# Unused products in TensorE's early gaps, and a regrouped hand-over from routing to the first expert

## The chip, the cores and the metric

The kernel runs on one core of one Trainium2 chip. A core has five engines that run their own instruction streams in order and meet through semaphores: PE (TensorE, matrix products), DVE (VectorE), ACT (ScalarE), POOL (GpSimd) and SP (SyncE, which here only issues DMAs). PE writes its results to PSUM, eight banks of 2 KB for each of the 128 partitions, from where the other engines read them. The metric is the time of one execution on the device in microseconds, less is better. Where several executions are timed, the median is given.

## The reference

Block-causal attention over 8x8 heads, and then a mixture of eight experts with a fixed capacity over its output. Cut to what matters:

```python
# attention: q, k, v are (8, 8, 576, 64) fp32
scores = (1 / sqrt(64)) * q @ k.transpose(0, 1, 3, 2)
scores = where(row // 64 >= col // 64, scores, -1e9)
attn = exp(scores - max(scores)); attn = attn / (sum(attn) + 1e-9)
attn_out = attn @ v
# experts: x is (4608, 512), 8 experts, cap = 576 tokens each
x = attn_out.transpose(0, 2, 1, 3).reshape(4608, 512)
logits = x @ w_gate
# (token, expert) pairs are visited from the largest logit down; a pair is
# taken if the token has no expert yet and the expert has fewer than cap
for e in range(8):
    out[assigned == e] = relu(x[assigned == e] @ w1[e]) @ w2[e]
```

w1 is 512x1024 and w2 1024x512 for each expert. Everything is fp32 from outside.

## The kernel before

The 64 heads are worked off as 32 pairs, two heads side by side in the 128 partitions. For a pair, PE computes the scores of a block of 128 rows (L380, in fp16 parts of q and k, `qT`, `kT`, `kS`), DVE takes the row maxima (L405), ACT the exponentials (L416), and POOL divides the probabilities `P` by the row sums (L438). PE then transposes `P` in 128x128 fp32 blocks (L463, in the order of row blocks t=6 to 0), ACT and DVE copy the transposed blocks `PT` out of PSUM (L444, L446), and PE multiplies them with the values `V` (L498). PSUM banks 4 to 7, called `'x'` in the code, hold the transposes and the value products; two pairs of banks, `'S'`, hold the scores.

Behind the attention come the experts. For expert k a search in 14 rounds finds the logit from which on tokens belong to it. A round is a chain over three engines: `ja` on ACT (L760) and `jk` on DVE (L791) count the tokens above trial thresholds, PE adds the counts over the partitions (`tot`, L807), and DVE picks the next thresholds (L810). The routing then turns the result into a list of row indices (`th` L821, `po` L893, `pe` L995, `ix` L1004). POOL gathers the rows of x by indirect DMA into `xg` (L1068), five pieces of 128 rows (the last has 64). For expert 0, PE transposes each piece (`xt`, L1079, eight blocks) and DVE and ACT copy the result into `X`; for the later experts SP issues transposing DMAs from `xg` into `X` (L1094). PE multiplies with w1 in three fp16 products for each of four slices of the 512 inputs (`h`, L1119). ACT writes relu(h) in fp16 as `HH` (L1105), DVE the rest as `HL` (L1107). PE multiplies these with w2 (`y`, L1145 and L1149), ACT scales (L1127) and POOL scatters the rows to the output (L1135). While expert k is multiplied, the rounds and the gather for expert k+1 run between.

`h` is computed in 8 blocks f of 128 hidden units. The 576 rows are cut in two parts: 128 and 448 for expert 0, 256 and 320 for the others. The name `h_f_part` says which block and part. Each block and part has a PSUM bank of its own out of four (tag `g`), and a first matmul that starts the bank anew and a last one that stops it, since 12 matmuls add up there.

Nothing in this order is written out by hand. A planner (`Sched`) holds a list of tasks, each with its engine, a cost in ns and the events that it waits for, plays them forward on a model of the engines, and emits the instruction of the task that can start next by rules of priority. The instruction stream of an engine is the order in which its tasks were emitted, so a cost or a landing time in the model changes the order of the work and nothing else. `x[0]` in the run loop is the planned start of a task, `s.free[T]` the planned time from which PE is free, `s.res['x']` the planned times at which the `'x'` banks come free. While the first gather is under way, PE multiplies constants ten times into an unused tile (`warm`, L968).

Of the kernel before, what the change touches and what calls it, by code (L numbers as in the profile page):

```python
# [8 lines left out]
F32 = mybir.dt.float32  # L9
F16 = mybir.dt.float16  # L10
I32 = mybir.dt.int32
AF = mybir.ActivationFunctionType
OP = mybir.AluOpType
AX = mybir.AxisListType
P = 128

D, A, T, G, S = "DATGS"
# [6 lines left out]
class Sched:  # L24
# [5 lines left out]
    def __init__(s):  # L30
        s.lanes = [0] * 8
        s.free = {e: 0 for e in "DATGS"}
        s.ev = {0: 0}
        s.rt, s.gn, s.tasks, s.now, s.n, s.q, s.hw, s.res, s.shape = 0, 0, [], 0, 0, 0, 0, {}, None

    def add(s, gen, prio, t):
        s.n += 1
# [79 lines left out]
    def run(s):  # L117
        while s.tasks:
            c = []
            for k in s.tasks:  # L120
                best = None
                bias = next((x for x in k[4][2:] if isinstance(x, float)), 0)
                for n, e in enumerate(k[4][0]):
                    t = s.start(k, e)
                    if t is None:
                        break
                    cost = k[4][1][n] if len(k[4][0]) > 1 else k[4][1]
                    b = max(t, s.free[e] if e != S or cost else 0)
                    b += s.TURN if e == T and any(isinstance(x, Shape) and x != s.shape for x in k[4][2:]) else 0
                    if n == 0 or b + cost + bias < best[0] + best[6]:  # L130
                        best = (b, k[0], k[1], k, t, e, cost)
                if best:
                    c.append(best)
            assert c, [(k[4], k[1]) for k in s.tasks]
            c.sort(key=lambda x: x[:3])
            for x in c:
                end = x[0] + x[6]
                if x[6] == 0 or x[0] - x[4] > s.WAIT or not any(y[1] < x[1] and y[5] == x[5] and y[0] < end - (s.ST if x[5] == T else s.SLACK) and y is not x for y in c):
                    break
            else:  # L140
                x = c[0]
            k, e, cost = x[3], x[5], x[6]
            s.now, s.lat, s.xlag, s.eng = x[0] + cost, True, 0, e
            if e != S or cost:
                s.free[e] = s.now
            if e == T:
                s.shape = next((x for x in k[4][2:] if isinstance(x, Shape)), s.shape)
            s.tasks.remove(k)
            k[2], k[3] = s.now, e
            try:  # L150
                op = next(k[5])
            except StopIteration:
                continue
            if not s.lat:
                k[3] = None
            k[2] += s.xlag
            k[4] = op
            s.tasks.append(k)


class Attn:
# [443 lines left out]
    PX, BX = 3, 0.0  # L605
    PR = dict(load_qk=5, load_v=6, split=7, swap=2, scores=5, transpose=6, values=8, rows=7, logits=5, gate=1)

    def start(s):
        sc = s.sc
        sc.res.update(S={0: 0, 1: 0}, x={4: 0, 5: 0, 6: 0, 7: 0})  # L610
        for nm, f in (('load_qk', s.load_qk()), ('split', s.split('q')), ('split', s.split('k')), ('swap', s.swap()), ('load_v', s.load_v()),
                      ('scores', s.scores()), ('transpose', s.transpose()), ('values', s.values()), ('rows', s.rows()), ('logits', s.logits()), ('gate', s.gate())):
            sc.add(f, s.PR[nm], 0)


class Moe:
# [443 lines left out]
    def gather(s,k,ix):  # L1060
        nc=s.nc; fp=s.fp; sc=s.sc
        tl=[]
        for m in range(5):
            n=P if m<4 else 64
            yield G,1038 if k else 1350,('ffn',k-2),('xm',k-1,m)
            if m==0: X=s.X[k]=fp.tile([P,8,576],F16,tag="X",name=f"X{k}")
            xg=fp.tile([P,1024],F16,tag="xg",name=f"xg{k}_{m}",bufs=5)
            nc.gpsimd.indirect_dma_start(out=xg[:n],out_offset=None,in_=s.xd,in_offset=bass.IndirectOffsetOnAxis(ap=ix[:n,m:m+1],axis=0))  # L1068
            sc.soft(728,('xg',k,m))
            if k==0: sc.ev['xg',k,m]=sc.now+3000  # L1070
            sc.nolat()
            if m==4: sc.set(('gi',k))
            sc.add(s.flip(k,m,n,xg,X),1,sc.now)
# [23 lines left out]
    def ffn(s,k):  # L1097
        nc=s.nc; fp=s.fp; sc=s.sc
        yield S,0,('xm',k,0),('xm',k,1 if k else 0),*[('wc',k,n) for n in range(4) if k or n==0]
        (W,Y),X=s.W[k],s.X[k]  # L1100
        HH=fp.tile([P,8,576],F16,tag="HH",name=f"HH{k}",bufs=1); HL=fp.tile([P,8,576],F16,tag="HL",name=f"HL{k}",bufs=1)
        def hev(f,h,ps,gk,ts):
            w=ts.stop-ts.start
            yield A,51+.835*w
            nc.scalar.activation(HH[:,f,ts],ps,AF.Relu)  # L1105
            yield D,69+1.042*w
            nc.vector.scalar_tensor_tensor(HL[:,f,ts],ps,0.0,HH[:,f,ts],op0=OP.max,op1=OP.subtract)  # L1107
            sc.set(('h',k,8*h+f)); sc.set(gk)
        for h,ts in enumerate((slice(0,256),slice(256,576)) if k else (slice(0,128),slice(128,576))):
            w=ts.stop-ts.start  # L1110
            for f0 in range(0,8,4):
                pg={}
                nf=4 if k==0 and h==0 and f0==0 else 1
                for f,d in [(f,d) for a in range(f0,f0+4,nf) for d in range(4) for f in range(a,a+nf)]:
                    yield T,3*(w/2.4+3),'g' if d==0 else None,('g2',k-1),*[('xm',k,m) for m in range(1,5) if h],('wc',k,d) if k==0 else None
                    if d==0: gk=sc.gtake(); pg[f]=s.ps.tile([P,512],F32,tag="g",name=f"h{k}_{f}_{h}",bufs=4)[:,:w],gk
                    ps,gk=pg[f]
                    for n,(a,l) in enumerate(((0,0),(0,2),(1,0))):
                        nc.tensor.matmul(ps,lhsT=W[:,a,d,f*P:f*P+P],rhs=X[:,4*(d//2)+d%2+l,ts],start=(d==0 and n==0),stop=(d==3 and n==2))  # L1119
                    sc.nolat()  # L1120
                    if d==3: sc.add(hev(f,h,ps,gk,ts),1,sc.now+200)
        sca=1.0/(s.XS*s.WS*s.WS)
        def yev(m,ps,gk):
            n=P if m<4 else 64
            yield A,478
            y=fp.tile([P,512],F32,tag="y",name=f"yo{k}_{m}",bufs=3)
            nc.scalar.activation(y[:n],ps[P-n:],AF.Copy,scale=sca)  # L1127
            if m==4:

                yield D,603  # L1130
                nc.vector.scalar_tensor_tensor(y[:n],ps[:n],sca,y[:n],op0=OP.mult,op1=OP.add)
            sc.set(gk)

            yield G,1038,('yo',s.ny-1),('gi',1) if k==0 and m>1 else None
            nc.gpsimd.indirect_dma_start(out=s.out,out_offset=bass.IndirectOffsetOnAxis(ap=s.ix[k][:n,m:m+1],axis=0),in_=y[:n],in_offset=None)  # L1135

            if m==4 and k>s.E-3: nc.gpsimd.drain()
            sc.soft(728,('yo',s.ny)); sc.ev['yo',s.ny]=max(sc.ev['yo',s.ny],sc.now+4500); s.ny+=1
        for m in range(5) if k+1<s.E else (0,1,2,4,3):
            if m==0: sc.set(('mid',k))  # L1140
            for f in range(8 if m<4 else 4):
                yield T,645 if m<4 else 720,*[(x,k,y) for g in ((f,) if m<4 else (f,f+4)) for x,y in (('h',g),('h',8+g),('wc',4+g//2))],'g' if f==0 else None
                if f==0: gk=sc.gtake(); ps=s.ps.tile([P,512],F32,tag="g",name=f"y{k}_{m}",bufs=4)
                for n,(Z,a) in enumerate(((HH,0),(HH,1),(HL,0))):
                    if m<4: nc.tensor.matmul(ps,lhsT=Z[:,f,m*P:m*P+P],rhs=Y[:,a,f],start=(f==n==0),stop=(f==7 and n==2))  # L1145
                    else:

                        for g in range(2):
                            nc.tensor.matmul(ps[64*g:64*g+64],lhsT=Z[:,4*g+f,512:576],rhs=Y[:,a,4*g+f],start=(f==n==0),stop=(f==3 and n==2))  # L1149
                sc.nolat()  # L1150
            if m==4: sc.set(('g2',k)); sc.set(('ffn',k))
            sc.add(yev(m,ps,gk),1,sc.now+200)
        if k+1<s.E: sc.add(s.ffn(k+1),3,sc.now)
# [10 lines left out]
def attention_moe_kernel(ctx, tc, q, k, v, wg, w1, w2, out):  # L1164
    nc = tc.nc
# [5 lines left out]
    x = dram.tile([N, 2 * H * D], F16, name="x")  # L1171
    sc = Sched()
    with tc.manual_schedule():
# [8 lines left out]
            sc.add(moe.consts(), 70, 0)  # L1182
            sc.run()
        with ExitStack() as inner:
            sc.SLACK, sc.ST, sc.WAIT = 150, 500, 300
            moe.pools(inner)
            moe.run()
# [25 lines left out]
```

## Time and profile before

| what | us |
|---|---|
| median of 3 runs | 773.67 (769.49 to 773.80) |
| the profiled execution, whole | 775.91 |
| its span from first to last instruction | 774.1 |

The profile is of one execution. Its span counts from the first instruction to the last, and the 1.8 us more of the whole execution lie around it. One run of three is 4 us faster than the others without any change of the program. The page shows for each engine the time that it is busy; the trace gives start and length of groups of instructions, and in brackets how long the engine was idle before such a group and what ended that wait. PE's granted clock is full or half, and the page shows it by slices.

| stage | us of the span |
|---|---|
| start-up and first head pairs | 0 to 32 |
| attention | 32 to 340 |
| logits' end, routing and gather for expert 0 | 340 to 375 |
| expert 0 and the routing for expert 1 | 375 to 425 |
| experts 1 to 7 | 425 to 774 |

### The profile page before, as it was taken

How to read it: one execution, taken by the hardware profiler on the slowest of the kernel's cores; microseconds unless marked ns; L12 is line 12 of the kernel's file. 1: busy time of each engine (PE TensorE's matmuls, PEld its weight loads, DVE VectorE, ACT ScalarE, POOL GpSimd, SP SyncE). 2: the span in 40 equal slices, each digit the busy share in tenths (PEclk: the TensorE clock that was granted, in tenths of full speed). 3: DMA queues.
4: the chain of work that ended last, by engine and by line, in shares of the span. 5: the costliest groups of instructions: out<-in, count | busy, mean ns of one | idle time of the engine just before them, and what ended most of it. 6: DMA issues, size and time to landing. Idle time of an engine off the chain costs nothing.

```text
span 774.1 us, 18968 instructions
## 1 busy us (share of the span) xinstructions
PE 715.2 (92%) x6496; PEld 475.2 (61%) x6496; DVE 560.7 (72%) x2290; ACT 537.0 (69%) x1451; POOL 467.9 (60%) x515
## 2 busy tenths in 40 slices
PE   5779998999989999966999999999999999999997
PEld 3656776667767777743545747647557475574753
DVE  6899888998889889758988978869678693420210
ACT  5688888888988899844835869594965947492211
POOL 5788977898889886714413447293761926766001
PEclk9899999999999999986999999999999999999999
DMA  9878999999999986245229276492935719752001
GB/s 203 165 151 164 214 196 215 175 152 228 187 214 173 229 195 110 78 118 188 106 80 225 98 245 157 166 204 71 279 88 184 184 40 286 254 157 76 28 14 48
DMA packets 249123, 122.84 MB, mean 159 GB/s; under 512 B 205601, under 2 KB 232097, under 8 KB 249025
## 3 DMA queue, kind: packets, MB, share of 16 engines
q1 hardware_dynamic: 243088, 102.60, 59.2%
q0 software_dynamic: 5936, 19.01, 8.0%
q8 instruction: 52, 0.85, 0.5%
q14 instruction: 47, 0.38, 0.2%
HBM read 71.45 MB, written 18.87 MB: 117 GB/s over the span
## 4 chain that ended last, share of the span: by engine, by line
PE 36%; DMA 8%; ACT 3%; POOL 2%; issue 2%; DVE 1%; SPq 1%; POOLq 0%; ACTq 0%; DVEq 0%
PE h L1119 20%; PE y L1145 13%; DMA raw<-in_moe_w_dram 4%; DMA xg<-x,ix 2%; PE y L1149 2%; DMA out_dram<-yo,ix 1%; DMA X<-xg 1%; POOL xg L1068 1%; ACT ja L760 1%; POOL W L1038 1%; ACT W L1036 1%; ACT raw L1032 1%; SPq L1094 1%; PE pe L995 0%; SPq L1008 0%
## 5 line engine op out<-in xcount | busy, mean ns | idle before, releaser
L438 POOL TENSOR_TENSOR P<-P,m 128x320 f32<-128x320 f32 (+8 forms) x285 | 209.6, 770 | 48.7 <-DVE m L430 32.3
L1119 PE MATMUL h<-X,W 128*128 128x320 f16 (+3 forms) x1536 | 195.5, 286 | 2.1 <-DMA X<-xg 1.9
L1119 PEld LDWEIGHTS <-W 128*128 128x128 f16 x1536 | 141.5, 98 | 43.6 <-issue 4.5
L416 ACT ACTIVATE P<-psb,m 128x576 f32<-128x576 f32 (+8 forms) x288 | 149.4, 543 | 25.8 <-DVE m L409 17.2
L1145 PE MATMUL y<-W,HH 128*128 128x512 f16 x512 | 152.3, 379 | 0.0
L405 DVE TENSOR_REDUCE m<-psb 128x1 f32<-128x576 f32 (+8 forms) x288 | 124.9, 481 | 12.6 <-PE psb L380 12.1
L1038 POOL TENSOR_TENSOR W<-raw,W 128x1024 f16<-128x1024 f32 x56 | 118.3, 2137 | 26.0 <-ACT W L1036 22.5
L463 PE MATMUL psb<-mident,P 128*128 128x128 f32 x800 | 107.3, 283 | 12.5 <-POOL P L438 5.7
L1135 POOL DMA_INDIRECT out_dram<-yo,ix x40 | 39.2, 980 | 115.1 <-ACT yo L1127 69.8
L380 PEld LDWEIGHTS <-qT 128*64 128x64 f16 x1408 | 77.1, 112 | 43.7 <-issue 29.2
L463 PEld LDWEIGHTS psb<-mident,P 128*128 128x128 f32 x800 | 88.5, 144 | 23.9 <-POOL P L438 8.4
L380 PE MATMUL psb<-kT,qT 128*64 128x288 f16 (+8 forms) x704 | 90.7, 284 | 11.1 <-ACT P L416 10.3
L498 PE MATMUL psb<-PT,V 128*64 128x448 f32 (+5 forms) x776 | 98.1, 391 | 2.1 <-DVE PT L446 1.6
L1145 PE MATMUL y<-W,HL 128*128 128x512 f16 x256 | 97.0, 379 | 0.0
L1105 ACT ACTIVATE HH<-h 128x320 f16<-128x320 f32 (+3 forms) x128 | 51.7, 407 | 62.4 <-PE h L1119 57.2
L1068 POOL DMA_INDIRECT xg<-x,ix x40 | 41.0, 1025 | 79.9 <-DMA raw<-in_moe_w_dram 32.2
L444 ACT ACTIVATE PT<-psb 128x512 f32<-128x512 f32 (+1 forms) x165 | 82.5, 593 | 5.3 <-PE psb L463 4.9
L1107 DVE SCALAR_TENSOR_TENSOR HL<-h,HH 128x320 f16<-128x320 f32 (+3 forms) x128 | 57.2, 452 | 37.5 <-ACT HH L1105 37.4
L380 PE MATMUL psb<-kS,qT 128*64 128x288 f16 (+8 forms) x704 | 82.8, 280 | 1.2 <-DVE kS L350 1.0
L1145 PEld LDWEIGHTS <-HH 128*128 128x128 f16 x512 | 46.9, 98 | 53.7 <-issue 2.6
L1032 ACT ACTIVATE raw<-raw 128x512 f32<-128x512 f32 x112 | 67.3, 624 | 9.8 <-DMA raw<-in_moe_w_dram 9.0
L498 PEld LDWEIGHTS psb<-PT,V 128*64 128x64 f32 x776 | 49.7, 138 | 33.3 <-issue 24.4
(239 smaller groups left out, 1027.9 us busy)
## 6 DMA issues: line engine op xcount, KB each, us to landing
raw<-in_moe_w_dram SPq DMA_DIRECT2D x64, 512.0 KB, 5.4
x<-XR SPq DMA_DIRECT2D x8, 1152.0 KB, 5.5
kn<-in_k_dram SPq DMA_DIRECT2D x15, 576.0 KB, 5.1
qn<-in_q_dram SPq DMA_DIRECT2D x15, 576.0 KB, 7.4
V<-in_v_dram SPq DMA_DIRECT2D x64, 128.0 KB, 4.1
V<-in_v_dram SPq DMA_DIRECT2D x16, 64.0 KB, 3.7
xg<-x,ix POOLq DMA_INDIRECT x41, 4.5
out_dram<-yo,ix POOLq DMA_INDIRECT x40, 3.6
```

Of the source, the lines that this page charges most:

```text
L380: nc.tensor.matmul(out if len(K1.shape) == 2 else out.rearrange("p (r j) -> p r j", r=2), lhsT=A[:, h, 64 * i:64 * i + 64], rhs=K1, start= ...
L405: nc.vector.tensor_reduce(m[:, 0, c:c + 1], ps[:, o:o + 64 * (i + 1)] if g else s.part(ps, g, i, o), axis=AX.X if g else AX.XY, op=OP.max)
L416: nc.scalar.activation(out, in_, AF.Exp, bias=m[:, 1, c:c + 1], scale=s.ESC, accum_out=m[:, 2, c:c + 1])
L438: nc.gpsimd.tensor_tensor(sl, sl, m[:, 3, c:c + 1].to_broadcast([P, w]), op=OP.mult)
L444: s.nc.scalar.activation(out, in_, AF.Copy)
L463: nc.tensor.transpose(ps[:, a], s.Pb[n % s.NP][:, s.OFF[i] + 128 * j:s.OFF[i] + 128 * j + P], s.ident)
L498: nc.tensor.matmul(ps[64 * h:64 * h + 64, 64 * (i0 - b0):64 * (b1 - b0)], lhsT=vn[:, j, 2 * (n % 2) + h, :], rhs=pt[:, s.PTI[(j, i0)]:s.PT ...
L1032: nc.scalar.activation(raw[:,x],raw[:,x],AF.Copy,scale=s.WS)
L1038: nc.gpsimd.tensor_tensor(lw,raw,hi,op=OP.subtract)
L1107: nc.vector.scalar_tensor_tensor(HL[:,f,ts],ps,0.0,HH[:,f,ts],op0=OP.max,op1=OP.subtract)
L1119: nc.tensor.matmul(ps,lhsT=W[:,a,d,f*P:f*P+P],rhs=X[:,4*(d//2)+d%2+l,ts],start=(d==0 and n==0),stop=(d==3 and n==2))
L1145: if m<4: nc.tensor.matmul(ps,lhsT=Z[:,f,m*P:m*P+P],rhs=Y[:,a,f],start=(f==n==0),stop=(f==7 and n==2))
```

## The change

Three edits. First, the planner gets a hook `fill`. It is called ahead of a PE task whose planned start lies between 13 and 30 us, if the planned gap on PE holds more than one unit of 215 ns and an `'x'` bank is free. It emits as many products of a 128x128 constant with a 128x512 broadcast of that constant into the free bank, and nothing reads them. It is switched off for the expert part.

```diff
+            if e == T and s.fill and 13000 < x[0] < 30000:
+                n, b = int((x[0] - s.free[T]) / 215), [t for t in s.res['x'] if s.res['x'][t] <= s.free[T]]
+                if n > 1 and b:
+                    s.fill(n, b[-1])
...
+    def fill(s, n, b):
+
+        for _ in range(n):
+            s.nc.tensor.matmul(s.bank(b), lhsT=s.moe.idh, rhs=s.moe.idh[:, None, :].to_broadcast([P, 4, P]), start=True, stop=True)
...
+        sc.fill = s.fill
...
-            sc.SLACK, sc.ST, sc.WAIT = 150, 500, 300
+            sc.SLACK, sc.ST, sc.WAIT, sc.fill = 150, 500, 300, None
```

Second, the planned cost of issuing expert 0's gathers and their planned landing become numbers for each piece:

```diff
-            yield G,1038 if k else 1350,('ffn',k-2),('xm',k-1,m)
+            yield G,1038 if k else (1350,1300,1900,2000,1750)[m],('ffn',k-2),('xm',k-1,m)
...
-            if k==0: sc.ev['xg',k,m]=sc.now+3000
+            if k==0: sc.ev['xg',k,m]=sc.now+(3700,2900,2350,2400,2600)[m]
```

Third, for expert 0's first 128 rows four blocks f share one PSUM bank, so that two evictions of 128x4x128 take the place of eight of 128x128 on ACT and on DVE. Only the first matmul of a bank starts it and only the last stops it:

```diff
-        def hev(f,h,ps,gk,ts):
-            w=ts.stop-ts.start
+        def hev(f,h,ps,gk,ts,nf):
+            w=nf*(ts.stop-ts.start); x=slice(f,f+nf)
             yield A,51+.835*w
-            nc.scalar.activation(HH[:,f,ts],ps,AF.Relu)
+            nc.scalar.activation(HH[:,x,ts],ps,AF.Relu)
             yield D,69+1.042*w
-            nc.vector.scalar_tensor_tensor(HL[:,f,ts],ps,0.0,HH[:,f,ts],op0=OP.max,op1=OP.subtract)
+            nc.vector.scalar_tensor_tensor(HL[:,x,ts],ps,0.0,HH[:,x,ts],op0=OP.max,op1=OP.subtract)
...
-                nf=4 if k==0 and h==0 and f0==0 else 1
+                nf=1 if k or h else 4
                 for f,d in [(f,d) for a in range(f0,f0+4,nf) for d in range(4) for f in range(a,a+nf)]:
+                    new=d==0 and (f-f0)%nf==0
...
+                    if new: gk=sc.gtake(); pf=s.ps.tile([P,512],F32,tag="g",name=f"h{k}_{f}_{h}",bufs=4)[:,:nf*w].rearrange("p (f t) -> p f t",f=nf)
...
-                        nc.tensor.matmul(ps,lhsT=W[:,a,d,f*P:f*P+P],rhs=X[:,4*(d//2)+d%2+l,ts],start=(d==0 and n==0),stop=(d==3 and n==2))
+                        nc.tensor.matmul(ps,lhsT=W[:,a,d,f*P:f*P+P],rhs=X[:,4*(d//2)+d%2+l,ts],start=(new and n==0),stop=(d==3 and n==2 and (f-f0+1)%nf==0))
```

In all, PE gets 20 unused products at four places of the first head pairs; otherwise no engine's order differs in the attention. Line numbers of the kernel after are higher: L380, L463, L498, L807, L1079 and L1119 of before are L384, L467, L502, L817, L1089 and L1130.

The third of the four places, on PE: the 128-wide scores of the second pair (`qT_171` is its q), and behind them the four transposes of row block t=5 of the first pair (`P_88`). Before:

```order
L380 LDWEIGHTS qT_171
L380 MATMUL psb<-kS_114,qT_171 64x128
L380 LDWEIGHTS qT_171
L380 MATMUL psb<-kS_114,qT_171 64x128
L463 MATMUL psb<-mident,P_88 128x128 x4
L380 LDWEIGHTS qT_171
L380 MATMUL psb<-kT_166,qT_171 64x320
```

After (L615 is the hook, `m_idh` the constant):

```order
L384 LDWEIGHTS qT_171
L384 MATMUL psb<-kS_114,qT_171 64x128
L615 LDWEIGHTS m_idh
L615 MATMUL psb<-m_idh 128x512
L615 LDWEIGHTS m_idh
L615 MATMUL psb<-m_idh 128x512
L615 LDWEIGHTS m_idh
L615 MATMUL psb<-m_idh 128x512
L615 LDWEIGHTS m_idh
L615 MATMUL psb<-m_idh 128x512
L467 MATMUL psb<-mident,P_88 128x128 x4
```

Four products now stand between the scores and the transposes. The other places are ahead of the transposes of t=6 of the first pair (4), between the 224-wide and the 512-wide scores of the second pair (7), and ahead of the first value product (5).

The hand-over to expert 0, on PE: before, the first three `h` products stand between the transposes of the gather's second piece (`xg_1`) and its third (`xg_2`). Before:

```order
L1079 LDWEIGHTS xg_1_5755
L1079 MATMUL xt_1_5812<-m_idh,xg_1_5755 128x128
L1119 LDWEIGHTS W_0_5742
L1119 MATMUL h_0_0_5833<-X_5744,W_0_5742 128x128
L1119 LDWEIGHTS W_0_5742
L1119 MATMUL h_0_0_5833<-X_5744,W_0_5742 128x128
L1119 LDWEIGHTS W_0_5742
L1119 MATMUL h_0_0_5833<-X_5744,W_0_5742 128x128
L1079 LDWEIGHTS xg_2_5780
L1079 MATMUL xt_2_5838<-m_idh,xg_2_5780 128x128
```

After:

```order
L1089 MATMUL xt_2_5850<-m_idh,xg_2_5800 128x128
L1089 LDWEIGHTS xg_2_5800
L1089 MATMUL xt_2_5850<-m_idh,xg_2_5800 128x128
L1130 LDWEIGHTS W_0_5762
L1130 MATMUL h_0_0_5869<-X_5764,W_0_5762 128x128
L1130 LDWEIGHTS W_0_5762
L1130 MATMUL h_0_0_5869<-X_5764,W_0_5762 128x128
```

The first `h` products moved behind the third piece. In groups, PE's order up to the first 448-wide product was xt_0, tot_0, xt_1, 3 h, xt_2, 9 h, xt_3, 9 h, xt_4, 6 h, tot_1, and then h with tot_2 behind 21 and tot_3 behind 33 more; it is now tot_0, xt_0, xt_1, xt_2, 12 h, xt_3, 12 h, tot_1, 6 h, xt_4, 27 h, tot_2, 36 h, tot_3, 3 h. These `tot` belong to the search for expert 1.

The start of expert 1, on PE: `y_4` is the end of expert 0, `tot_3` the fourth round of the search for expert 2, and `h_0_0` the first product of expert 1, with its rows `X` and weights `W_1`. Before:

```order
L1149 MATMUL y_4_6659<-W_0_5743,HL_5830 64x512
L807 LDWEIGHTS m_bo
L807 MATMUL tot_3_6705<-cn_3_6678,m_bo 128x3
L1119 LDWEIGHTS W_1_6414
L1119 MATMUL h_0_0_6711<-X_6539,W_1_6414 128x256
```

After:

```order
L1160 MATMUL y_4_6650<-W_0_5763,HL_5860 64x512
L1130 LDWEIGHTS W_1_6422
L1130 MATMUL h_0_0_6709<-X_6547,W_1_6422 128x256
L1130 LDWEIGHTS W_1_6422
L1130 MATMUL h_0_0_6709<-X_6547,W_1_6422 128x256
L1130 LDWEIGHTS W_1_6422
L1130 MATMUL h_0_0_6709<-X_6547,W_1_6422 128x256
L817 LDWEIGHTS m_bo
L817 MATMUL tot_3_6714<-cn_3_6686,m_bo 128x3
```

`tot_3` moved behind the first three products of expert 1. In the later experts `tot` and other small steps stand at other places among the products in the same way.

More of the change, by code (lines that the diff above doesn't have):

```diff
@@ L33, in __init__ @@
         s.ev = {0: 0}
-        s.rt, s.gn, s.tasks, s.now, s.n, s.q, s.hw, s.res, s.shape = 0, 0, [], 0, 0, 0, 0, {}, None
+        s.rt, s.gn, s.tasks, s.now, s.n, s.q, s.hw, s.res, s.shape, s.fill = 0, 0, [], 0, 0, 0, 0, {}, None, None
     def add(s, gen, prio, t):
@@ L1101, in ffn @@
         HH=fp.tile([P,8,576],F16,tag="HH",name=f"HH{k}",bufs=1); HL=fp.tile([P,8,576],F16,tag="HL",name=f"HL{k}",bufs=1)
-        def hev(f,h,ps,gk,ts):
-            w=ts.stop-ts.start
+        def hev(f,h,ps,gk,ts,nf):
+            w=nf*(ts.stop-ts.start); x=slice(f,f+nf)
             yield A,51+.835*w
-            nc.scalar.activation(HH[:,f,ts],ps,AF.Relu)
+            nc.scalar.activation(HH[:,x,ts],ps,AF.Relu)
             yield D,69+1.042*w
-            nc.vector.scalar_tensor_tensor(HL[:,f,ts],ps,0.0,HH[:,f,ts],op0=OP.max,op1=OP.subtract)
-            sc.set(('h',k,8*h+f)); sc.set(gk)
+            nc.vector.scalar_tensor_tensor(HL[:,x,ts],ps,0.0,HH[:,x,ts],op0=OP.max,op1=OP.subtract)
+            for i in range(f,f+nf): sc.set(('h',k,8*h+i))
+            sc.set(gk)
         for h,ts in enumerate((slice(0,256),slice(256,576)) if k else (slice(0,128),slice(128,576))):
@@ L1111, in ffn @@
             for f0 in range(0,8,4):
-                pg={}
-                nf=4 if k==0 and h==0 and f0==0 else 1
+                nf=1 if k or h else 4
                 for f,d in [(f,d) for a in range(f0,f0+4,nf) for d in range(4) for f in range(a,a+nf)]:
-                    yield T,3*(w/2.4+3),'g' if d==0 else None,('g2',k-1),*[('xm',k,m) for m in range(1,5) if h],('wc',k,d) if k==0 else None
-                    if d==0: gk=sc.gtake(); pg[f]=s.ps.tile([P,512],F32,tag="g",name=f"h{k}_{f}_{h}",bufs=4)[:,:w],gk
-                    ps,gk=pg[f]
+                    new=d==0 and (f-f0)%nf==0
+                    yield T,3*(w/2.4+3),'g' if new else None,('g2',k-1),*[('xm',k,m) for m in range(1,5) if h],('wc',k,d) if k==0 else None
+                    if new: gk=sc.gtake(); pf=s.ps.tile([P,512],F32,tag="g",name=f"h{k}_{f}_{h}",bufs=4)[:,:nf*w].rearrange("p (f t) -> p f t",f=nf)
+                    ps=pf[:,(f-f0)%nf]
                     for n,(a,l) in enumerate(((0,0),(0,2),(1,0))):
-                        nc.tensor.matmul(ps,lhsT=W[:,a,d,f*P:f*P+P],rhs=X[:,4*(d//2)+d%2+l,ts],start=(d==0 and n==0),stop=(d==3 and n==2))
+                        nc.tensor.matmul(ps,lhsT=W[:,a,d,f*P:f*P+P],rhs=X[:,4*(d//2)+d%2+l,ts],start=(new and n==0),stop=(d==3 and n==2 and (f-f0+1)%nf==0))
                     sc.nolat()
-                    if d==3: sc.add(hev(f,h,ps,gk,ts),1,sc.now+200)
+                    if d==3 and (f-f0+1)%nf==0: sc.add(hev(f-nf+1,h,pf,gk,ts,nf),1,sc.now+200)
         sca=1.0/(s.XS*s.WS*s.WS)
```

## The prediction

> **What bounds the kernel now.** I read the page's engine shares and clock row first, then busy time by stage, then the clock around each dip, the matmul timeline there, and last the hand-over from routing to the experts. On the page the second number is TensorE's (PE's) share of the span, and PEclk gives the granted clock of each fortieth of it in tenths:
>
> ```profile
> PE 715.2 (92%) x6496; PEld 475.2 (61%) x6496; DVE 560.7 (72%) x2290; ACT 537.0 (69%) x1451; POOL 467.9 (60%) x515
> PEclk9899999999999999986999999999999999999999
> ```
>
> Stretches that I cut at the start-up, the attention, the routing, expert 0 and the other experts; columns: length, busy time of PE, its weight loads, DVE, ACT and POOL, then granted clock, DMA share, GB/s:
>
> ```profile
> 0.00:32.00 32.00, 18.98 (x160) 14.16 (x162) 21.33 (x68) 20.63 (x55) 18.52 (x48) 0.89 0.93 177
> 32.00:340.00 308.00, 287.31 (x3271) 215.00 (x3267) 265.17 (x884) 260.42 (x801) 247.02 (x324) 0.99 0.88 175
> 340.00:375.00 35.00, 19.82 (x232) 12.96 (x230) 30.62 (x146) 17.32 (x41) 10.49 (x12) 0.76 0.67 210
> 375.00:425.00 50.00, 48.09 (x321) 24.67 (x319) 42.86 (x214) 28.47 (x67) 18.25 (x13) 1.00 0.49 114
> 425.00:774.10 349.10, 340.99 (x2521) 208.38 (x2519) 200.69 (x983) 210.15 (x490) 173.59 (x118) 1.00 0.50 144
> ```
>
> PE is the bound at 93% of 32 to 340 and 98% of 425 to 774; it idles in the first 32 us and the 35 us of routing. The change works at these two seams. What it saves there counts only if the PE-bound stretch behind it starts earlier.
>
> The clock first. Windows cut to fit its steps; columns: length, PE busy, granted clock, DMA share, GB/s:
>
> ```profile
> 19.78:23.20 3.42, 1.62 (x14) 1.00 0.26 43
> 23.20:26.61 3.41, 2.40 (x19) 0.50 0.68 130
> 26.61:30.02 3.41, 3.41 (x17) 0.50 1.10 203
> 47.09:50.50 3.41, 1.85 (x26) 1.00 1.06 195
> 50.50:53.92 3.42, 3.42 (x22) 0.50 1.11 260
> 419.14:422.55 3.41, 1.83 (x18) 1.00 1.21 185
> ```
>
> The steps lie on one grid of 3.41 us, whatever the kernel does. A window with PE busy 1.62 or 1.85 us is followed by one at half clock; the page's clock row shows no step behind the 1.83 in 419 to 423. After a full window (26.61 to 30.02, 50.50 to 53.92) the clock is back. So I put the threshold near 1.84 us of work, that is, about 1.57 us of idle within one window.
>
> The matmuls around the first dip (start, duration, in brackets the idle ahead and what ended it), and POOL's normalising beside them:
>
> ```profile
> 18.10 0.33 PE L463 MATMUL psb<-mident,P 128*128 128x128 f32 x1 [0.79 <-POOL P L438]
> 20.92 0.41 PE L380 MATMUL psb<-kT,qT 128*64 128x512 f16 x2 [1.49 <-ACT P L416]
> 22.23 0.44 PE L463 MATMUL psb<-mident,P 128*128 128x128 f32 x2
> 24.09 0.69 PE L463 MATMUL psb<-mident,P 128*128 128x128 f32 x2 [1.42 <-POOL P L438]
> 26.42 4.25 PE L463 MATMUL psb<-mident,P 128*128 128x128 f32 x21
> 31.55 2.92 PE L498 MATMUL psb<-PT,V 128*64 128x128 f32 x24 [0.88 <-DVE PT L446]
> 36.85 2.40 PE L463 MATMUL psb<-mident,P 128*128 128x128 f32 x20
> 22.65 7.00 POOL L438 TENSOR_TENSOR P<-P,m 128x512 f32<-128x512 f32 x9 [2.27 <-DVE m L430]
> ```
>
> At half clock the block of transposes takes 4.25/21 = 202 ns each; at full clock (36.85) 120 ns.
>
> **Part 1: the unused products.** Twenty of 128x512 fp16, at four places: 4 ahead of the transpose at 18.10, 7 ahead of the 512-wide scores at 20.92, 4 ahead of the two transposes at 22.23, 5 ahead of the first value product at 31.55. The nearest row is the y product with 512 columns:
>
> ```profile
> 412.33 0.59 PE L1145 MATMUL y<-W,HH 128*128 128x512 f16 x2
> 412.98 0.59 PE L1145 MATMUL y<-W,HH 128*128 128x512 f16 x2
> ```
>
> Three products (two with HH, one with HL) start between these, 0.65/3 = 0.217 us each. The four groups cost 0.87, 1.52, 0.87 and 1.08 us. The idle they stand in is 0.79, 1.49, 1.42 and 0.88 us, so they overrun by 0.08, 0.03, nothing and up to 0.20. The third group is covered because the next two transposes wait for POOL until 24.09 anyway; without POOL's wait it would cost its 0.87. The products read a constant and write a free bank of PSUM, so no DMA and no other engine works for them, and nothing waits for them but the PE rows behind.
>
> With 19.78 to 23.20 filled, its busy time goes from 1.62 to about 1.62+1.52+0.87, the whole window but for what the phase moves; no step at 23.20. Then the 21 transposes take 21x0.120 = 2.52 us and not 4.25. They still begin at 26.42, because POOL's last multiply of the pair sets that. They end at 28.94; the last PSUM copy ran 0.88 behind, so the values could start at 29.82, and the fifth group's 1.08 us plus the transpose ahead of it (0.12 us) puts it at about 30.2. Against 31.55 that is 1.3 us earlier. Is it kept? The largest of PE's waits in 32 to 340, grouped by what they are for (sum, times, longest):
>
> ```profile
> PE psb L380 <- ACT P L416: 7.3, 15, 1.0
> ```
>
> It is on an engine that moves along with PE; no DMA is among the others. I count the whole **-1.3 us**. Bounds: 0 if a dip stays, -1.7 (21x0.082) if nothing else stood in the way; the value taken lies between, by the values' own start.
>
> The weak point is the grid: it runs free, so its place in another execution is any. Before, nearly every place of a 3.41-us window catches too little work somewhere in 17 to 30. After, only 23 to 26.4 remains thin: 0.6 us idle ahead of 24.09, then some 0.2 ahead of 26.42, and scores that take at full clock half of what they show. A window from about 23.0 to 26.4 holds some 1.7 us and would still trip, which I estimate for a quarter of the places.
>
> [...]
>
> **Parts 2 and 3: the hand-over.** The planned issue costs and landing times of expert 0's gathers emit nothing; they alone reorder. Four blocks per bank make 2 evictions of 128x4x128 on ACT and on DVE out of 8 of 128x128. ACT's by form, with sum in us and mean in ns:
>
> ```profile
> L1105 ACT ACTIVATE HH<-h 128x128 f16<-128x128 f32 x8 | 1.8, 269 | 0.0
> L1105 ACT ACTIVATE HH<-h 128x448 f16<-128x448 f32 x8 | 4.3, 538 | 0.0
> ```
>
> From 128 to 448 columns ACT grows 0.84 ns a column, so 512 take 592 ns, and two of them 1.2 us against 2.2 (8x0.269). DVE has as many evictions of the same shapes, which I take to save as much. Neither is the bound in 375 to 425, so the 1.0 us each only relieves the routing beside them. On PE the order counts:
>
> ```profile
> 366.50 0.62 PE L1079 MATMUL xt<-m_idh,xg 128*128 128x128 f16 x8 [1.02 <-DMA xg<-x,ix]
> 368.45 0.41 PE L1079 MATMUL xt<-m_idh,xg 64*128 64x64 f16 x8 [0.82 <-DMA xg<-x,ix]
> 371.13 0.16 PE L807 MATMUL tot<-cn,m_bo 128*128 128x3 f16 x1 [0.62 <-ACT ja L760]
> 371.41 2.00 PE L1119 MATMUL h<-X,W 128*128 128x128 f16 x33
> 373.27 2.14 PE L1119 MATMUL h<-X,W 128*128 128x128 f16 x21
> ```
>
> 33 h products take 2.00 us, 61 ns each. Before, 81 of the 96 narrow ones stand ahead of the row at 373.27 and 15 follow, so the 448-wide ones start at 373.27+15x0.061 = 374.2. After, the gathers land as before (nothing ahead of them moved), 12 products fit in the gap ahead of 368.45 and 6 more behind tot_1; past 368.86 remain 66, 4.0 us, and two tots whose inputs have arrived: 373.1. So PE is 1.1 us ahead. Is that kept? Rows of the next route and of expert 1's start:
>
> ```profile
> 395.42 0.18 PE L807 MATMUL tot<-cn,m_bo 128*128 128x3 f16 x1
> 406.84 1.00 POOL L1068 DMA_INDIRECT xg<-x,ix x1 [0.77 <-DVE ix L1004]
> 412.90 7.78 DMA X<-xg
> 418.63 0.18 PE L807 MATMUL tot<-cn,m_bo 128*128 128x3 f16 x1
> 420.72 1.80 PE L1119 MATMUL h<-X,W 128*128 128x256 f16 x15 [1.91 <-DMA X<-xg]
> 422.35 0.17 PE L807 MATMUL tot<-cn,m_bo 128*128 128x3 f16 x1
> ```
>
> Expert 1 begins when its gathered rows land, and these hang on route 1, a chain of small steps on ACT, DVE and PE whose rounds keep their pace: I place its last tot at 395.5 to 395.6, not earlier. So the 1.1 us turns into a longer wait: **+0.1**. The wait grows from 1.9 to about 3.2 us, also because tot_3 of route 2, at 418.63 ahead of the wait before, now stands behind three products of expert 1. Route 2's next rounds on ACT and DVE wait for it. A round takes (395.42-371.13)/11 = 2.2 us; from tot_3 at about 421.1 (three products of 1.80/15 = 0.12 us behind 420.72) tot_4 comes at 423.3 and not 422.35, so the route runs about 1 us late. Expert 2's first h stands without a wait at
>
> ```profile
> 471.01 0.83 PE L1119 MATMUL h<-X,W 128*128 128x256 f16 x6
> ```
>
> so up to 1.0 us of wait may appear there; between 0 and 1.0 I take **+0.3**, nearer the lower end because PE did not wait there at all.
>
> A wait of 3.2 us holds over 1.57 us of one window wherever the grid lies, so it trips; the half clock then costs half a window of products, 1.7 us. Before, 1.9 us of wait trips where 1.57 fall in one window, which counted over all places is about 64 in 100. The change adds 0.36x1.7 = **+0.6**.
>
> Sum: -1.3+0.1+0.3+0.6 = -0.3 us. The profiled execution took 775.91 us, 2.2 above the median of 773.67 of the three runs shown; there the sum gives 775.6, and on the median 773.4.
>
> **Rivals.** (1) The hand-over's gain survives: if expert 1's indices are found earlier, because DVE and ACT are relieved by 1.0 us, X lands 1.1 earlier, the wait stays at 1.9 and nothing new trips: -1.3-1.1+0.3 = -2.1, 771.6. Against it: the chain waits for the round before, not for evictions. (2) The fills do nothing for the clock: the dip moves to the thin window ahead of 26.4 and the transposes stay at 202 ns; only the hand-over counts, +1.0, and the time is 774.7. For it: 1.62 and 1.85 tripped. (3) Slower by the clock at expert 1 alone: if before hardly ever trips there, as its 1.83 us of work did not, while 3.2 us of wait always does, the whole 1.7 is new: -1.3+0.4+1.7 = +0.8, 774.5. It decides from 1.57 us of idle in one window. Expert 2's wait at its upper bound adds 0.7 more, 775.2.
>
> **How the numbers follow.** The forecast 0.45, rival 1 0.2, rival 2 0.2, rival 3 0.15. The cases lie between 771.6 and 775.2, closer together than the three runs shown (769.49 to 773.8); since places of the grid differ by whole dips of 1.7 us from run to run, I widen by about 2 below and 1 above: 769.5 to 776.0. A measurement of this kernel tells about 1%, 7.7 us, from no change. Every case is within it: same 0.94, and 0.03 to each side for what I have not seen.
>
> **What would show it.** Right: no half clock between 23 and 30, 21 transposes in about 2.5 us and the first value product 1.3 earlier; 20 new matmuls of 0.22 us; 448-wide products from about 1.1 us earlier against the attention's end; the wait for X about 3 us and a half-clock window behind it. Wrong: a dip one window later than before, an attention that ends no earlier though its start does, X landing earlier, or a wait for X at expert 2.

## The result, and the profile after

The changed kernel took 783.23, 782.45 and 779.46 us; a fourth run, of 3469.35 us, was disturbed and is left out of the ratio, though it counts in the median of 782.84. Before took 773.02 (median of four runs here). The ratio is 1.0114, 95% interval 1.0082 to 1.0146: slower by about 1.1%, where 773.4 and no difference were forecast. The profiled execution is 783.23 us, its span 781.4 against 774.1, so 7.3 us of the loss lie inside the span.

The page's PE row and clock row after:

```profile
PE 719.5 (92%) x6516; PEld 476.5 (61%) x6516; DVE 556.0 (71%) x2284; ACT 536.4 (69%) x1445; POOL 467.0 (60%) x515
PEclk9999999999999999967999997999999999999999
```

The dip of the second slice is gone. A new one stands in slice 25, at 469 to 488 us, where before had none: the seam between expert 1 and expert 2.

First the attention. PE's timeline there (start, duration, and in brackets the idle ahead with what ended it):

```profile
15.93 0.33 PE L384 MATMUL psb<-kT,qT 128*64 128x320 f16 x2 [1.74 <-ACT P L420]
...
25.94 2.72 PE L467 MATMUL psb<-mident,P 128*128 128x128 f32 x21 [1.06 <-POOL P L442]
28.50 1.24 PE L615 MATMUL psb<-m_idh 128*128 128x512 f16 x5
29.67 1.57 PE L502 MATMUL psb<-PT,V 128*64 128x128 f32 x10
```

The 21 transposes took 2.72 us (4.25 before), and the first value product starts at 29.67 instead of 31.55. Of these 1.88 us, 0.48 were there before any unused product (these scores started at 16.41 before), so the products are worth about 1.4 here. In the profile with 33 products, in the last of the runs below, the first value product starts at 29.48.

How early the routing starts is read from the first POOL instruction behind the attention, a memset (first row before, second after, each from POOL's timeline):

```profile
340.71 0.13 POOL L673 MEMSET m_PB<- 128x36 f32 x1 [11.54 <-issue]
```
```profile
337.60 0.13 POOL L683 MEMSET m_PB<- 128x36 f32 x1 [11.55 <-issue]
```

The attention ends 3.1 us earlier: the 1.9 us above, and 1.2 more. Where the 1.2 come from isn't shown. Before has a half-clock window from 132.4 to 135.8 that this execution lacks, but a later run without the unused products lacks it too and has this memset at 341.58. In the nine profiles with the 20 products it lies between 337.35 and 339.39.

The hand-over and the start of expert 1, PE's timeline:

```profile
370.06 2.03 PE L1130 MATMUL h<-X,W 128*128 128x128 f16 x12
...
417.81 0.80 PE L1130 MATMUL h<-X,W 128*128 128x256 f16 x3 [3.17 <-DMA X<-xg]
```

Of the 12 products at 370.06 three are narrow, so the 448-wide ones start at 370.2, 4.0 us before the old 374.2: 3.1 of these come from the attention and 0.9 from the new order. Expert 1 starts at 417.81, 2.9 us earlier. The 0.9 became wait, as forecast.

All of PE's waits between 430 and the end (what for; sum, times, longest). Before, this list had one entry, for tot, 1.7 us in all:

```profile
PE tot L817 <- ACT ja L770: 5.2, 4, 3.0
PE h L1130 <- POOL W L1048: 3.2, 1, 3.2
```

The two long ones stand next to each other, at the start of expert 2:

```profile
472.32 0.16 PE L817 MATMUL tot<-cn,m_bo 128*128 128x3 f16 x1 [2.99 <-ACT ja L770]
472.35 2.51 PE L1130 MATMUL h<-X,W 128*128 128x256 f16 x11
478.06 2.32 PE L1130 MATMUL h<-X,W 128*128 128x256 f16 x10 [3.21 <-POOL W L1048]
```

PE is done with expert 1 and the tot behind it at 469.33, waits 2.99 us for tot_6 of the search for expert 3, and 11 products later 3.21 us for a slice of expert 2's weights. The clock there, in windows cut on its steps (length, PE busy, granted clock, DMA share, GB/s):

```profile
414.35:417.76 3.41, 0.30 (x4) 1.00 0.72 183
417.76:421.17 3.41, 3.35 (x17) 0.50 1.13 177
468.96:472.37 3.41, 0.42 (x7) 1.00 0.71 214
472.37:475.79 3.42, 2.49 (x12) 0.50 0.96 250
475.79:479.20 3.41, 1.14 (x6) 0.50 0.20 77
479.20:482.61 3.41, 3.41 (x19) 0.50 0.00 0
```

One half-clock window behind the wait for X at expert 1, three at expert 2. From expert 1's start to expert 3's it took 530.76-417.81 = 112.95 us, against 521.52-420.72 = 100.80 before. Of these 12.15 us the waits are 3.0+3.2. The half clock is taken to cost half of the busy time in its windows (an h product takes 2.51/11 = 0.23 us at 472.35, and 2.45/21 = 0.12 at full clock in the row of before below): 3.35/2 = 1.7 at expert 1 and (2.49+1.14+3.41)/2 = 3.5 at expert 2. Together that is 11.4; the other 0.8 are not traced. Expert 3 to the end is 1.9 us shorter than before. So -2.9+12.15-1.9 = +7.3, the difference of the spans.

Why a slice of weights comes late is seen in POOL's timeline at that seam, before and after. L1038 and L1048 are conversions of weight slices, L1135 and L1146 scatters of expert 1's output. Before:

```profile
461.30 2.14 POOL L1038 TENSOR_TENSOR W<-raw,W 128x1024 f16<-128x1024 f32 x1
463.60 1.01 POOL L1135 DMA_INDIRECT out_dram<-yo,ix  x1 [0.17 <-ACT yo L1127]
464.64 6.30 POOL L1038 TENSOR_TENSOR W<-raw,W 128x1024 f16<-128x1024 f32 x3
471.11 1.00 POOL L1135 DMA_INDIRECT out_dram<-yo,ix  x1 [0.17 <-issue]
476.20 0.96 POOL L1135 DMA_INDIRECT out_dram<-yo,ix  x1 [4.09 <-ACT raw L1032]
```

After:

```profile
461.02 1.00 POOL L1146 DMA_INDIRECT out_dram<-yo,ix  x1 [0.30 <-issue]
462.05 6.32 POOL L1048 TENSOR_TENSOR W<-raw,W 128x1024 f16<-128x1024 f32 x3
468.53 1.00 POOL L1146 DMA_INDIRECT out_dram<-yo,ix  x1 [0.17 <-ACT raw L1042]
474.89 0.96 POOL L1146 DMA_INDIRECT out_dram<-yo,ix  x1 [5.36 <-ACT ja L770]
475.88 4.21 POOL L1048 TENSOR_TENSOR W<-raw,W 128x1024 f16<-128x1024 f32 x2
```

Before, all four slices of expert 2's first weights are converted by 470.94. PE's products there:

```profile
471.01 0.83 PE L1119 MATMUL h<-X,W 128*128 128x256 f16 x6
471.71 2.45 PE L1119 MATMUL h<-X,W 128*128 128x256 f16 x21
```

The slices are multiplied in order, three products each, and only the third of a slice reads the part that POOL converts. So slice 3 is first needed by the twelfth product, the sixth of the second row, at about 472.3: 1.3 us behind its conversion. After, it is the twelfth product too that waits until 478.06, behind the 11 shown above. The planner now put the scatter of piece 1 ahead of slice 0, and those of pieces 2 and 3 ahead of slice 3. Between the two scatters POOL stands still for 5.36 us, and slice 3 is finished at about 478.0. ACT is named as the releaser, but it had written piece 3 by 467.3; in a later run, where slice 3 stands between the same two scatters, the trace names the write of the scatter before as what the next one waits for (0.23 us). Here the trace has that write landing 5.6 us behind its issue, at 474.1, and the scatter of piece 3 starts 0.8 us behind the landing. The same pause stands in the profile before (4.09 us): the write lands 4.3 us behind its issue, at 475.4, and the next scatter again starts 0.8 us behind that. There, nothing that PE needed at once was queued behind it.

The wait for tot_6 hangs on ACT:

```profile
470.48 0.63 ACT L1042 ACTIVATE raw<-raw 128x512 f32<-128x512 f32 x1 [1.05 <-DMA raw<-in_moe_w_dram]
471.13 0.59 ACT L1138 ACTIVATE yo<-y 64x512 f32<-64x512 f32 x1
471.63 0.55 ACT L770 ACTIVATE ja<-m_PB,cd 128x324 f16<-128x324 f32 x1
```

`ja` of that round is queued behind a conversion step whose raw weights are late, and PE's row of tot_6 now stands ahead of expert 2's first product (before, behind the first six).

### The profile page after: what moved, and what is told of

Its sections match the earlier page's. It is cut to its first block, busy times and chain, and to the rows that moved or that the text cites. A ratio compares the mean times of both kernels' runs of the same rounds, so it can differ in the third digit from the quotient of the medians.

```text
span 781.4 us, 18999 instructions
## 1 busy us (share of the span) xinstructions
PE 719.5 (92%) x6516; PEld 476.5 (61%) x6516; DVE 556.0 (71%) x2284; ACT 536.4 (69%) x1445; POOL 467.0 (60%) x515
## 4 chain that ended last, share of the span: by engine, by line
PE 39%; DMA 5%; ACT 4%; issue 3%; POOL 2%; DVE 2%; POOLq 0%; SPq 0%; ACTq 0%; DVEq 0%
PE h L1130 23%; PE y L1156 12%; DMA raw<-in_moe_w_dram 2%; PE y L1160 2%; ACT W L1046 1%; DMA out_dram<-yo,ix 1%; ACT ja L770 1%; DMA X<-xg 1%; POOL W L1048 1%; ACT raw L1042 1%; PE warm L978 1%; PE pe L1005 1%; POOL xg L1078 1%; DMA xg<-x,ix 1%; ACT yo L1138 0%
## 5 line engine op out<-in xcount | busy, mean ns | idle before, releaser
L1130 PE MATMUL h<-X,W 128*128 128x320 f16 (+3 forms) x1536 | 199.9, 290 | 6.4 <-POOL W L1048 3.2
L1130 PEld LDWEIGHTS <-W 128*128 128x128 f16 x1536 | 143.9, 99 | 51.9 <-issue 4.5
L1048 POOL TENSOR_TENSOR W<-raw,W 128x1024 f16<-128x1024 f32 x56 | 118.1, 2132 | 24.7 <-ACT W L1046 24.1
L467 PE MATMUL psb<-mident,P 128*128 128x128 f32 x800 | 104.9, 279 | 11.5 <-POOL P L442 5.3
L1146 POOL DMA_INDIRECT out_dram<-yo,ix x40 | 39.2, 981 | 118.4 <-ACT yo L1138 71.4
L384 PEld LDWEIGHTS <-qT 128*64 128x64 f16 x1408 | 76.0, 111 | 41.9 <-issue 27.3
L467 PEld LDWEIGHTS psb<-mident,P 128*128 128x128 f32 x800 | 86.5, 141 | 22.9 <-POOL P L442 7.4
L384 PE MATMUL psb<-kT,qT 128*64 128x288 f16 (+8 forms) x704 | 89.4, 281 | 11.4 <-ACT P L420 10.0
L1115 ACT ACTIVATE HH<-h 128x256 f16<-128x256 f32 (+3 forms) x122 | 51.2, 420 | 70.2 <-PE h L1130 63.8
L502 PE MATMUL psb<-PT,V 128*64 128x448 f32 (+5 forms) x776 | 97.2, 388 | 0.9 <-DVE PT L450 0.4
L1117 DVE SCALAR_TENSOR_TENSOR HL<-h,HH 128x256 f16<-128x256 f32 (+3 forms) x122 | 56.6, 467 | 41.5 <-ACT HH L1115 41.4
L384 PE MATMUL psb<-kS,qT 128*64 128x288 f16 (+8 forms) x704 | 81.7, 277 | 0.1
L502 PEld LDWEIGHTS psb<-PT,V 128*64 128x64 f32 x776 | 49.3, 137 | 32.3 <-issue 24.4
```

The lines of the kernel that those rows point to most:

```text
L384: nc.tensor.matmul(out if len(K1.shape) == 2 else out.rearrange("p (r j) -> p r j", r=2), lhsT=A[:, h, 64 * i:64 * i + 64], rhs=K1, start= ...
L467: nc.tensor.transpose(ps[:, a], s.Pb[n % s.NP][:, s.OFF[i] + 128 * j:s.OFF[i] + 128 * j + P], s.ident)
L502: nc.tensor.matmul(ps[64 * h:64 * h + 64, 64 * (i0 - b0):64 * (b1 - b0)], lhsT=vn[:, j, 2 * (n % 2) + h, :], rhs=pt[:, s.PTI[(j, i0)]:s.PT ...
L1048: nc.gpsimd.tensor_tensor(lw,raw,hi,op=OP.subtract)
L1117: nc.vector.scalar_tensor_tensor(HL[:,x,ts],ps,0.0,HH[:,x,ts],op0=OP.max,op1=OP.subtract)
```

## The experiments

In each, "the change" is the changed kernel. Medians are of the runs of one batch on one chip; the ratio to the runs of before on that chip is what is compared. It is an estimate over the runs of a batch with its 95% interval (in brackets), and can differ from the quotient of the two medians by up to 0.4%. Unused products change no output.

**Which part loses.** Theory: the loss is the order that the planner writes for the seam of experts 1 and 2, and it comes with the four-block banks. Rivals: an earlier start that runs into late weight loads (A), the gather times (B), the clock alone (C).

The unused products alone: gather times and `hev`/`ffn` as before.

> Only the unused products of part 1; gather times and banks as before. Theory (the loss comes from the order that the four-block banks make the planner write for expert 2): the attention's gain stays and nothing is lost, so the first gather is issued 1.5 to 3 us earlier than 357.8 and the time is 1 to 3 us under before, about 771; the first weight slices of expert 2 are converted before its first product. Rival A (an earlier start runs into weight loads that land no earlier): the gain is lost again by expert 2, time as before or up to 8 us more, with a wait for W there.

Measured: 775.92 against 776.97, ratio 0.9968 (0.9941 to 0.9995). The attention's end is at 339.39, 1.3 us earlier than 340.71, and there is no wait for W. Part 1 is a small gain by its ratio, with an interval just clear of 1, while the medians are only 1.0 us apart. As the cause of the loss rival A falls. That the gain is lost again, its other half, isn't refuted: in this profile the gain is gone by expert 2, whose first product starts at 471.34, against 471.01 before.

The gather times and banks alone:

```diff
-        sc.fill = s.fill
+        sc.fill = None
```

> Only the gather times and the four-block banks, without the unused products. Theory: the same two waits at expert 2 as in the changed kernel (about 3 us for tot, 3 us for W of the fourth slice) and the same half clock around them, so 9 to 12 us over before, about 784. Rival A (the early start matters, not the order): without the attention's gain the waits shrink below 2 us in all and the time is within 4 us of before.

Measured: 787.64 against 776.97, ratio 1.0102 (1.0067 to 1.0137). PE's waits around the seam, the longest two of its profile:

```profile
PE h L1130 <- POOL W L1048: 6.5, 1, 6.5
PE tot L817 <- ACT ja L770: 3.7, 4, 1.8
```

The loss is there without the unused products, against the rival of an early start. The wait for W is 6.5 us, more than the 3 expected, and the longest for tot 1.8, less than expected. The interval of this ratio and that of the change (1.0082 to 1.0146) overlap widely, so what the unused products are worth inside the changed kernel isn't settled by these runs.

Unused products and gather times, banks of before:

> Unused products and gather times, banks as before. Its order at experts 1 and 2 on PE and POOL is that of before. Theory: as with the unused products alone, about 771, within 1 us of that run. Rival B (the gather times do the harm): 780 or more.

Measured: 774.79 against 776.97, ratio 0.9964 (0.9938 to 0.9991). The gather times do no harm; rival B falls.

Unused products and banks, gather times of before:

> Unused products and four-block banks, with the gather times of before. Theory (the banks alone make the planner write the bad order; on POOL and PE it is the same at expert 2 as in the changed kernel): within 2 us of the changed kernel, 1.0% over before, with a wait for W of 3 us or more. Rival B (it takes the gather times as well): within 3 us of before.

Measured: 782.12 against 774.70, ratio 1.0098 (1.0067 to 1.0130), wait for W 4.5 us. The four-block banks bring the loss, without the new gather times here and without the unused products above. The traces say the same of the order: on POOL it is that of before, instruction for instruction, in the two runs without the four-block banks, and that of the change in the two with them. Why the planner moves the scatters when it has four-block banks stays open.

**Which step of the order loses.** All scatters of expert 1 behind the conversions:

```diff
-            yield G,1038,('yo',s.ny-1),('gi',1) if k==0 and m>1 else None
+            yield G,1038,('yo',s.ny-1),('gi',1) if k==0 and m>1 else None,('wc',2,0 if m==1 else 3) if k==1 and m>0 else None
```

> The whole change, and the scatters of expert 1's rows are planned no earlier than the conversion of expert 2's weights (piece 1 behind slice 0, pieces 2 to 4 behind slice 3). Theory: slice 3 is converted by about 470 instead of 478, the wait for W is gone, and with it its half clock: 6 to 9 us under the changed kernel, 773 to 777; what stays is the half clock at expert 1. Rival C (the clock alone costs it: PE idle at expert 1 and expert 2 anyway): within 2 us of the changed kernel, 781 or more.

Measured: 775.33 against 776.97, ratio 0.9971 (0.9950 to 0.9992). No wait for W, the longest wait for tot is 1.4 us, and two half-clock windows (418.37 to 425.20) remain behind a wait of 4.0 us for X at expert 1. An extra condition on one kind of task takes back the whole loss, with the banks still in place; rival C falls.

Only pieces 2 to 4 pinned (`('wc',2,3) if k==1 and m>1`):

> The whole change, with one pin: the scatters of pieces 2 to 4 of expert 1 are planned behind the conversion of slice 3 of expert 2's first weights; piece 1 still goes ahead of slice 0. Theory (slice 3 queued on POOL behind two scatters is the main loss): no wait for W, 5 to 9 us under the changed kernel. Rival D (the scatter of piece 1 ahead of slice 0 is the main loss, since it delays the weight loads and with them ACT): within 3 us of the changed kernel.

Measured: 773.68 against 773.48, ratio 0.9991 (0.9969 to 1.0012). Slice 3 is the main thing; the scatter of piece 1 ahead of slice 0 is worth little by itself, against rival D.

Only pieces 3 and 4 pinned (`m>2`), so that slice 3 stands between the scatters of pieces 2 and 3:

> The whole change, with one pin less than before: only the scatters of pieces 3 and 4 of expert 1 are planned behind the conversion of slice 3; the scatter of piece 2 stays ahead of it. Theory (POOL stands still in front of the scatter of piece 3 until the write of piece 2 has landed, and slice 3 is queued behind that): slice 3 follows the issue of piece 2 directly, is converted by about 472, and the wait for W is under 1 us; the time is within 2 us of the run with pieces 2 to 4 pinned. Rival F (any scatter ahead of slice 3 does it, by POOL's own time): half of the loss stays, 776 to 779.

Measured: 773.77 against 774.70, ratio 0.9997 (0.9965 to 1.0030). POOL's timeline at the seam:

```profile
459.12 6.32 POOL L1048 TENSOR_TENSOR W<-raw,W 128x1024 f16<-128x1024 f32 x3
465.61 1.00 POOL L1146 DMA_INDIRECT out_dram<-yo,ix  x1 [0.17 <-ACT raw L1042]
466.64 4.22 POOL L1048 TENSOR_TENSOR W<-raw,W 128x1024 f16<-128x1024 f32 x2
471.09 0.98 POOL L1146 DMA_INDIRECT out_dram<-yo,ix  x1 [0.23 <-DMA out_dram<-yo,ix]
```

Slice 3 starts the moment the scatter of piece 2 is issued. The scatter of piece 3 starts 5.48 us behind that of piece 2; in between POOL converts slice 3 and one more slice, and the 0.23 us that it still idles are put down to the write of piece 2. One scatter ahead of slice 3 costs 1 us of POOL and no more; it is the second one, with its wait for the first one's write, that costs. Rival F falls.

Only tot_6 of the search for expert 3 behind the first products of expert 2:

```diff
-                    yield T,30,('sg',k,t)
+                    yield T,30,('sg',k,t),('hs',2) if k==3 and t==6 else None
...
+                    if f==d==h==0: sc.set(('hs',k))
```

> The whole change, with only tot_6 of the search for expert 3 planned behind the first products of expert 2; POOL's order stays that of the changed kernel. Theory: the wait of 3.0 us for tot_6 goes, but the products then wait longer for slice 3 (to about 478 as before), so the gain is 0 to 2 us, with a wait for W of 5 to 6.5 us. Rival E (tot_6 ahead of the products is the cause): 3 to 6 us under the changed kernel.

Measured: 781.90 against 773.48, ratio 1.0115 (1.0082 to 1.0148). PE's waits around the seam:

```profile
PE h L1131 <- POOL W L1048: 5.3, 1, 5.3
PE h L1131 <- DMA X<-xg: 3.8, 2, 2.5
```

The wait for tot is gone and the wait for W has grown by 2.1 us; no time is won, against rival E. POOL's order is that of the change up to 505 us, behind this seam. Of the two waits in the changed kernel, 2.1 of the 3.0 us for tot were inside the time that PE would have waited for slice 3 anyway.

**The clock.** Twelve unused products ahead of expert 1's first product, in the changed kernel:

```diff
+                    if f==d==h==0 and k==1:
+                        wu=s.ps.tile([P,512],F32,tag='xt',name='warm1',bufs=2)
+                        for _ in range(12): nc.tensor.matmul(wu,lhsT=s.ones,rhs=s.iom.rearrange('p a b -> p (a b)')[:,:512],start=True,stop=True)
```

> The whole change, with 12 unused products of 128x512 on PE ahead of expert 1's first product, where PE waits 3.2 us for X. Theory (the half clock behind that wait costs 1.7 us): no half clock between 414 and 425, 1 to 2 us under the changed kernel. Rival: the wait is no longer than the products or expert 2 takes it back, within 1 us of the changed kernel.

Measured: 780.44 against 773.48, ratio 1.0087 (1.0061 to 1.0114); the clock of its profile is full from the routing's end to 471. The sign is as expected and 0.27% of 773 us is 2.1 us, but the intervals of this run and of the change overlap: it fits the 1.7 us and doesn't prove them.

All scatters pinned, these twelve products, and unused products in planned gaps up to 52 us (25 in all):

> The whole change with the scatters pinned as in the run that pinned them all, the 12 unused products ahead of expert 1, and unused products in planned gaps up to 52 us instead of 30 (25 instead of 20). If the dip near 50 and the one at expert 1 are what is left: 2 to 4 us under the run with the pinned scatters alone, 5 to 7 under before. If the dip near 50 stays: 1 to 2 us under it.

Measured: 772.12 against 773.48, ratio 0.9970 (0.9948 to 0.9991), no better than the pinned scatters alone (0.9971), so neither case that was expected came. In its profile the dip near 50 and the one at expert 1 are gone, and another has come:

```profile
19.81:23.22 3.41, 3.34 (x24) 1.00 0.23 42
23.22:26.64 3.42, 1.75 (x23) 1.00 0.69 133
26.64:30.05 3.41, 3.41 (x18) 0.50 1.10 205
```

The window of the old dip is full, but the next one fell on the thin place ahead of the transposes, and these ran at half clock as before the change. That takes back at most 1.7 us, by the prediction's estimate of 0.082 us for each of the 21; where the rest of the expected gain went stays open.

Last, the banks of before with the gather times, products up to 52 us, and four where the planner sees room for one:

```diff
-            if e == T and s.fill and 13000 < x[0] < 30000:
+            if e == T and s.fill and 13000 < x[0] < 52000:
...
+                n = 4 if n == 1 else n
```

> Banks of before; gather times of the change; unused products in planned gaps up to 52 us, and 4 where the planner sees a gap for one, among others ahead of the transposes at 26.4, where a window could still fall thin. If the dips near 23 to 30 and near 50 are what the fills are worth: no half clock ahead of the routing, 3 to 5 us under before. If the dip near 50 stays or the products overrun their gaps: 1 to 2.5 us under before.

Measured: 768.75 against 774.70, ratio 0.9923 (0.9892 to 0.9953). Stretches of its profile (length; busy time of PE; granted clock; DMA share; GB/s):

```profile
12.00:32.00 20.00, 17.48 (x162) 1.00 0.91 178
...
47.00:60.00 13.00, 9.81 (x104) 1.00 1.00 160
60.00:336.00 276.00, 260.94 (x3020) 1.00 0.93 179
```

No half clock ahead of the routing, which begins at 336.0, 4.7 us earlier than before. This is the fastest version measured, ahead of before and of the change: 33 products instead of 20, and the four-block banks left out.

## Why the prediction was wrong, point by point

**Right: the unused products.** 1.4 us on PE against 1.3 forecast; the run with them alone has a ratio of 0.9968, 2.5 us of 775, with an interval from 0.4 to 4.6 us. That the whole of it is kept, as the sum had it, isn't shown: in the profile of that run it was gone by expert 2, and the span is 774.0 against 774.1. The thin window ahead of 26.4, given as the weak point with one place in four, tripped, that is, was followed by a window at half clock, in one of the ten profiles with unused products that show the clock there (1.75 us of work at 23.22, 25 products). It held in the nine others, among them this one:

```profile
23.56:26.98 3.42, 1.83 (x23) 1.00 0.80 153
26.98:30.39 3.41, 3.41 (x27) 1.00 1.07 202
```

That is the run with pieces 2 to 4 pinned. So rival 2 is real in one execution of ten. The grid's place differs between executions, as was said: in eleven profiles cut into its windows of 3.41 us every window up to 766 us is at 1.00 or 0.50, and the grid begins between 0.09 us of the span (the run with the twelve products) and 3.08 (the one with pieces 2 to 4 pinned). That its place alone decided isn't shown.

**Right: the hand-over.** 0.9 us ahead instead of 1.1, kept as wait: 3.17 us for X against 3.2 forecast. Half clock behind it in the profiled execution (417.76 to 421.17), estimated above at 1.7 us. Rival 1 did not happen. Rival 3 named a place that did lose time, but a small part of it.

**Wrong: "so up to 1.0 us of wait may appear there" at expert 2, taken as +0.3.** This step looked at one way for expert 2 to be late, its rows X. X was not late there. The lateness came through POOL's queue and cost 9.7 us: waits of 3.0 and 3.2, and 3.5 of half clock by the estimate above. The prediction followed the moved rows on PE (tot, h, y) through experts 1 and 2 and not those on POOL, though the order of POOL differed at the same seam and expert 2's weights pass through it. In the profile before, slice 3 was converted at 470.94 and first needed at about 472.3: a slack of 1.3 us, which the list of waits does not show, since a wait of zero isn't listed. A delay on POOL beyond that had to become a wait of PE, and in the change slice 3 was finished at 478.0, 7.1 us later. So the step that failed is the one that counted expert 2's wait by X alone, at most 1.0 us, and put the wait for its weights at nothing without a reason.

**Wrong: the threshold.** "About 1.57 us of idle within one window" held in the attention, roughly: 1.75 tripped there, 1.83 did not in one profile, and 1.85 did before the change. Among the experts it was too strict. Unused products with gather times, where a wait of 3.1 us for X fell across a step:

```profile
415.28:418.69 3.41, 1.96 (x19) 1.00 1.05 103
418.69:422.10 3.41, 1.75 (x17) 1.00 1.16 181
422.10:425.51 3.41, 3.41 (x35) 1.00 0.89 172
```

There is no dip behind the 1.96 or the 1.75 us of work. So a wait of that length does not trip "wherever the grid lies": 3.17 us within one window did in the changed kernel, 3.1 us split over two did not. The term of +0.6 leaned on that and was too sure; it doesn't decide the result.

**The range** reached to 776.0 because every case ended within 1.8 us of the forecast. All of them priced seams that the diff names. None priced the seam that the planner had rewritten on POOL.

## What to carry to other kernels

Where a planner writes the order, a local edit can pay or lose far behind itself: compare the order of every engine at every later seam, above all the in-order queue of an engine that serves both urgent and patient work, and look for an instruction that waits for a DMA with urgent work queued behind it. A start without a wait is not slack: for each seam, look at when each input was ready and at which instruction first reads it. When the loss is found, pin the one pair of tasks that matters, as the scatters here, and keep the rest; and measure the parts of a change one by one, since here one part gained and another lost.

## What the runs showed of the hardware

- The granted clock did not follow PE's busy time alone. With about the same work in a window the attention's products tripped and the experts' did not: 1.75 us at 23.22 to 26.64 in one run, 1.75 us at 418.69 to 422.10 in another. Over the eleven profiles cut into such windows, the most work in a window that still tripped was 1.86 us in the attention (45.71 to 49.12 in the change) and 1.40 us among the experts (467.72 to 471.13 in the run with the twelve products); the least that held was 1.82 and 1.71 us (13.74 to 17.16 in the run with the twelve products; 466.96 to 470.37 in the run with all scatters pinned, the twelve products and 25 in planned gaps). Outside these two stages a window with 2.21 us tripped, across the attention's end (335.84 to 339.25 in the change), and one with 0.38 us held, in the start-up (2.71 to 6.13 before). Why they differ wasn't tried; the rows differ in shape, 128*64 and fp32 in the attention, 128*128 in fp16 among the experts.
- Behind the first of two waits of 3 us close together (2.99 and 3.21) the clock was at half for 10.2 us (472.37 to 482.61): the window behind the one with 2.49 us of work at half clock was still at half.
- At this seam the next scatter with no other work of POOL between started 5.1 us (before) and 6.4 us (the change) behind the one ahead of it, 0.8 us behind the landing of that one's write; before, nothing that PE needed at once was queued behind that pause; in the change slice 3 was, and PE waited 3.21 us for it.
